# Gate and residual mixes as one pair of row halves in a slot of the gate and value ring

## The chip, the cores and the metric

The kernel runs on one core of one Trainium2 chip. The metric is the device time of one execution in microseconds (us), the median of several runs. Ratios are the mean time of one kernel's fast runs over that of the kernel before in the same rounds, so they are not quite the ratio of the medians quoted. Engines: PE (matmuls), DVE (vector), ACT (scalar and activations), POOL (general), SP (issues transfers).

## The reference, cut to what matters

An attention through 32 inducing points, then a gated feed-forward layer on 49,664 tokens of 128 channels (`mab(q, kv)` is a softmax attention of q over kv):

```
h   = mab(inducing, x)            # per batch of 4: 32 x 128
x   = mab(x, h)                   # weights rt (tokens x 32), times h
g   = x @ w_gate ; val = x @ w_val            # 128 -> 1536
ffn_out  = gelu(g) * val @ w_out              # 1536 -> 128
res_gate = sigmoid(x @ w_res)
out = x + res_gate * ffn_out
```

The kernel never forms x of the second attention for the big products: as x = rt @ h, it folds h into the weights (`hg`, `hv`, `hr`) and multiplies them by `rt`. Two small products per group remain, the *mixes*: `rt @ hr` for the gate (as a tanh) and `rt @ ha` for the residual.

## The kernel before

A group is 512 tokens. It has six gate and six value tiles of 128 x 1024, in a ring of three PSUM tiles of two banks each. The other two of the eight banks, the side banks, hold the output sums of even and odd groups, and, when free, the mixes and other small work.

```python
ps_gv = ...tile_pool(name="psgv", bufs=3, space=PSUM)       # the ring
ps_2 = [...tile_pool(name=f"ps{i}", bufs=1, space=PSUM) for i in range(2)]

def side_bank(group): return ps_2[group % 2].tile(...)
def misc_bank():      return side_bank(parity[0] + 1)
def wide_bank():      return ps_gv.tile([P, 2 * TOK], ...)

def gate_slot(gi, si):            # v: two 64-row matmuls, one per row half
    v = slot_mms(gi, si, hg_t)
    act.activation(ge[:, :n], v, AC.Gelu, ...)                # L331
def value_slot(gi, si):
    v = slot_mms(gi, si, hv_t)                                # L322
    ve.tensor_tensor(u[:, :n], ge_t.pop((gi, si)), v, AL.mult) # L338
# class Last, one per group
def mms(self, n): ...             # 8 of 48 output matmuls, L361
def mix(self, h):                 # L370, rows 0 to 63
    bank = side_bank(self.gi + 1)
    r = slice(0, 2 * M)
    for k in range(self.nk):
        pe.matmul(bank[:, k * P:(k + 1) * P], rt...[r, self.j0 + k, :], h[r, :], ...)
def gate(self):      ...tanh of mix(hr) into th               # L378
def residual(self):  ...copy of mix(ha) into at               # L384
def end(self):
    ve.scalar_tensor_tensor(th, th, 1.0, ffn, AL.add, AL.mult)  # L389
    po.tensor_tensor(at, at, th, AL.add); sy.dma_start(out..., at)
...
# f: the group's first window; one gate, one value and one window per step
for i in range(6):
    at(f + 2 + i, lambda lg=lg: lg.mms(8))
at(f + 5, lg.gate, START)
at(f + 6, lg.residual, START)
at(f + 7, lg.end, LATE)
```

A window is the place in the program's order behind each value, where other pieces of work are put. Gates run up to four ahead of values. In a window the pieces go in the order START, MIDDLE, END, LATE. In batches 0 to 2 the groups also carry work for the next batch: a burst of exponentials, then sums in the side banks (`accumulate`, L172), then a second burst. A quiet stretch is one without such work, above all in batch 3.

The softmax here doesn't subtract the row's maximum and nothing guards it: scores larger than these inputs give would overflow.

## Time and profile before

| | before |
|---|---|
| median of 3 runs | 857.97 us (857.3 to 858.31) |
| a quiet group, start to start of L389 | 7.76 us |
| DVE's own work in it (6 x 1.131 + 0.598) | 7.39 us |

Here are the busy times of one quiet group, from L389 to the next L389 (the columns are the length, then each engine's busy time and its number of instructions).

```profile
core 0: us, PE busy (x) PEld busy (x) DVE busy (x) ACT busy (x) POOL busy (x), PEclk, DMA share, GB/s
749.79:757.55 7.76, 7.52 (x83) 4.47 (x82) 7.56 (x9) 6.97 (x9) 1.27 (x1) 1.00 0.09 35
```

PE and DVE both look 97% busy. But the recorded time of an instruction reaches into the next one: DVE starts a product every 1.131 us although each lasts 1.21. Start to start is what counts here. The view of waits has PE's value and gate matmuls wait little for ACT:

```profile
PE gv L322 <- ACT ge L331: 11.7, 34, 1.1
```

### The profile page before, as it was taken

To read this page: it belongs to the slowest core of one execution; us is meant where nothing else is said; L and a number is where in the kernel's file an instruction comes from. 1 tells how busy PE (TensorE), PEld (TensorE's weight loads), DVE (VectorE), ACT (ScalarE), POOL (GpSimd) and SP (SyncE) were. 2 spreads that over 40 slices of the span, in tenths; PEclk is the share of its full clock that TensorE was granted. 3 is DMA by queue.
4 is the path that set the end of the run, shared out by engine and by line. 5 is a ranking of instruction groups with operands and counts; after the bars stand their busy time and mean duration, and the time that the engine had idled before them with its cause. 6 is when DMAs were issued, how large, how long until landed. Compare 5 with 4: busy or idle time off the path is not lost.

```text
span 855.8 us, 23356 instructions
## 1 busy us (share of the span) xinstructions
PE 795.1 (93%) x9602; PEld 479.1 (56%) x9602; DVE 796.7 (93%) x784; ACT 734.1 (86%) x861; POOL 356.9 (42%) x313
## 2 busy tenths in 40 slices
PE   5889999999899999999989999999989999999997
PEld 4545556555555555555555555555555555555554
DVE  8699999899999999899999999989999999999997
ACT  5599998888889989888989998988888999988994
POOL 2538885111468766112247867311245611111111
PEclk9599999999999999999999999999999999999999
DMA  8337874010447765101245876200135501010111
GB/s 308 110 85 157 207 176 121 27 38 27 84 96 165 182 172 127 40 26 38 51 88 106 221 163 161 74 31 27 38 64 100 116 26 39 38 39 27 38 38 41
DMA packets 123787, 79.42 MB, mean 93 GB/s; under 512 B 102016, under 2 KB 104736, under 8 KB 123680
## 3 DMA queue, kind: packets, MB, share of 16 engines
q1 hardware_dynamic: 121392, 75.50, 35.4%
q10 hardware_dynamic: 2288, 2.43, 1.0%
q8 instruction: 75, 1.23, 0.7%
q14 instruction: 32, 0.26, 0.1%
HBM read 27.87 MB, written 25.43 MB: 62 GB/s over the span
## 4 chain that ended last, share of the span: by engine, by line
PE 52%; DVE 25%; issue 11%; ACT 8%; DMA 1%; POOL 1%; DVEq 0%; ACTq 0%; POOLq 0%; SPq 0%
PE gv L322 26%; DVE u L338 19%; PE sb L361 19%; ACT ge L331 6%; PE sb L370 5%; DVE lo L123 2%; DVE th L389 1%; DVE z L275 1%; DVE hi L121 1%; PE sb L172 1%; ACT at L384 1%; ACT th L378 1%; DMA ge<-in_moe_w_out_dram 1%; PE sb L174 0%; POOL wO L450 0%
## 5 line engine op out<-in xcount | busy, mean ns | idle before, releaser
L338 DVE TENSOR_TENSOR u<-ge,gv 128x1024 bf16<-128x1024 f32 x584 | 691.1, 1213 | 41.8 <-PE gv L322 26.0
L331 ACT ACTIVATE ge<-gv 128x1024 f32<-128x1024 f32 x584 | 591.7, 1023 | 79.3 <-PE gv L322 67.0
L361 PE MATMUL sb<-wO,u 128*128 128x128 bf16 x4656 | 360.5, 220 | 0.1
L361 PEld LDWEIGHTS <-u 128*128 128x128 bf16 x4656 | 262.1, 98 | 121.4 <-issue 98.9
L392 POOL TENSOR_TENSOR at<-at,th 128x512 f32<-128x512 f32 (+1 forms) x100 | 123.8, 1238 | 407.6 <-ACT ge L331 369.4
L322 PE MATMUL gv<-rt,hv 64*128 64x512 f16 x1152 | 222.5, 378 | 25.6 <-ACT ge L331 9.7
L322 PE MATMUL gv<-rt,hg 64*128 64x512 f16 x1152 | 224.9, 385 | 11.7 <-DVE u L338 6.9
L322 PEld LDWEIGHTS <-hv 64*128 64x128 bf16 x1200 | 99.5, 94 | 103.0 <-issue 88.6
L322 PEld LDWEIGHTS <-hg 64*128 64x128 bf16 x1200 | 63.9, 93 | 76.6 <-issue 16.8
L289 POOL TENSOR_TENSOR a<-e,z 128x1024 f16<-128x1024 f32 (+2 forms) x50 | 91.2, 1832 | 20.8 <-ACT e2s L268 12.9
L370 PEld LDWEIGHTS <-rt 64*128 64x128 f16 x768 | 56.7, 93 | 37.9 <-issue 17.6
L123 POOL TENSOR_TENSOR lo<-xf,hi 128x1024 f16<-128x1024 f32 x36 | 76.8, 2134 | 0.3
L389 DVE SCALAR_TENSOR_TENSOR th<-th,sb 128x512 f32<-128x512 f32 (+1 forms) x100 | 66.4, 664 | 1.8 <-PE sb L361 1.8
L378 ACT ACTIVATE th<-sb 128x512 f32<-128x512 f32 (+1 forms) x100 | 57.9, 579 | 8.8 <-PE sb L370 8.6
L384 ACT ACTIVATE at<-sb 128x512 f32<-128x512 f32 (+1 forms) x100 | 58.0, 580 | 0.8 <-PE sb L370 0.8
L121 POOL CAST hi<-xf 128x1024 f16<-128x1024 f32 x36 | 37.3, 1037 | 22.6 <-DMA xf<-in_x_dram 19.1
L370 PE MATMUL sb<-ha,rt 64*128 64x128 f16 x384 | 36.5, 214 | 0.2
L370 PE MATMUL sb<-hr,rt 64*128 64x128 f16 x384 | 36.6, 215 | 0.0
L148 PEld LDWEIGHTS <-xt 128*128 128x128 f16 x768 | 23.8, 98 | 3.3 <-issue 2.3
L139 ACT ACTIVATE xt<-gv 128x1024 f16<-128x1024 f16 x12 | 12.3, 1024 | 13.4 <-PE gv L138 13.3
L138 PE MATMUL gv<-identF,hi 128*128 128x128 f16 x96 | 11.2, 288 | 9.0 <-DVE hi L121 8.9
L268 ACT ACTIVATE e<-gv 128x1024 f32<-128x1024 f32 (+2 forms) x13 | 11.9, 959 | 7.8 <-PE gv L148 7.8
(93 smaller groups left out, 259.0 us busy)
## 6 DMA issues: line engine op xcount, KB each, us to landing
out_dram<-at SPq DMA_DIRECT2D x96, 256.0 KB, 2.1
xf<-in_x_dram SPq DMA_DIRECT2D x42, 512.0 KB, 4.2
ge<-in_x_dram SPq DMA_DIRECT2D x6, 512.0 KB, 5.8
rt<-a SPq DMA_TRANSPOSE x49, 3.1
xt<-hi SPq DMA_TRANSPOSE x36, 3.3
ge<-in_moe_w_gate_dram ACTq DMA_DIRECT2D x1, 512.0 KB, 4.8
ge<-in_moe_w_val_dram ACTq DMA_DIRECT2D x1, 512.0 KB, 4.3
ge<-in_moe_w_out_dram ACTq DMA_DIRECT2D x1, 512.0 KB, 4.4
```

What stands on the lines that cost most here:

```text
L121: e_hi.tensor_copy(hi[:, :w, :], xf[:, :w, :])
L123: e_lo.tensor_tensor(lo[:, :w, :P], xf[:, :w, :], hi[:, :w, :], AL.subtract)
L289: po.tensor_tensor(a2[:, :n], ev[:, o:o + n, :].unsqueeze(2).to_broadcast([P, n, Q, M]), z[:, 1, o:o + n].unsqueeze(2).unsqueeze(3).to_bro ...
L322: pe.matmul(v[:, c * tw:(c + 1) * tw], weights[b][r, (c0 + c) * P:(c0 + c + 1) * P], rt[r, :], start=True, stop=True)
L331: act.activation(ge[:, :n], v, AC.Gelu, bias=0.0, scale=1.0)
L338: ve.tensor_tensor(u[:, :n], ge_t.pop((gi, si)), v, AL.mult)
L361: pe.matmul(self.ffn[:, k, :], u_t[self.gi, si][:, o:o + P], wO[:, fc, :], start=first, stop=not self.todo, skip_group_check=True)
L370: pe.matmul(bank[:, k * P:(k + 1) * P], rt_t[self.b, self.k][r, self.j0 + k, :], h[r, :], start=True, stop=True)
L378: act.activation(self.th[:, :self.tw], bank[:, :self.tw], AC.Tanh, bias=0.0, scale=0.5)
L384: act.activation(self.at[:, :self.tw], bank[:, :self.tw], AC.Copy, bias=0.0, scale=1.0)
L389: ve.scalar_tensor_tensor(self.th[:, :tw], self.th[:, :tw], 1.0, self.ffn.rearrange("p k c -> p (k c)")[:, :tw], AL.add, AL.mult)
L392: po.tensor_tensor(self.at[:, :tw], self.at[:, :tw], self.th[:, :tw], AL.add)
```

## The change

The intent is to take the two mixes out of PE's way, run them in both row halves at once, and read them while DVE is on the final product. The mixes get a tile of the ring of their own, one window earlier than the group's first output matmuls.

```diff
-        po.tensor_tensor(ha[M:2 * M, :], hf[M:2 * M, :], ha[M:2 * M, :], AL.subtract)
+        po.tensor_tensor(ha[3 * M:, :], hf[3 * M:, :], ha[3 * M:, :], AL.subtract)
...
-        def mix(self, h):
-            bank = side_bank(self.gi + 1)
-            ... (and gate(), residual(), each with its own mix)
+        def mix(self):
+            bank = wide_bank()
+            n = self.tw
             for k in range(self.nk):
+                for r, o, h in ((slice(0, 64), 0, hr_t), (slice(64, 128), TOK, ha_t)):
+                    pe.matmul(bank[:, o + k * P:o + (k + 1) * P],
+                              rt_t[self.b, self.k][r, self.j0 + k, :], h[self.b][r, :], ...)
+            act.activation(self.th[:, :n], bank[:, :n], AC.Tanh, bias=0.0, scale=0.5)
+            act.activation(self.at[:, :n], bank[:, TOK:TOK + n], AC.Copy, ...)
...
+        at(f + 1, lg.mix, END)
...
-            at(f + 5, lg.gate, START)
-            at(f + 6, lg.residual, START)
... (and the two like them for the short group at the end of a batch)
```

In the kernel after, the lines are L372 (mix), L376 (tanh), L378 (copy), L382 (final product) and L385 (POOL's sum).

More of the change, by code (lines that the diff above doesn't have):

```diff
@@ L364, in mms @@
                     del u_t[self.gi, si]
-        def mix(self, h):
-            bank = side_bank(self.gi + 1)
-            r = slice(0, 2 * M)
+        def mix(self):
+            bank = wide_bank()
+            n = self.tw
             for k in range(self.nk):
-                pe.matmul(bank[:, k * P:(k + 1) * P],
-                          rt_t[self.b, self.k][r, self.j0 + k, :],
-                          h[r, :], start=True, stop=True)
-            return bank
-        def gate(self):
-            bank = self.mix(hr_t[self.b])
+                for r, o, h in ((slice(0, 64), 0, hr_t), (slice(64, 128), TOK, ha_t)):
+                    pe.matmul(bank[:, o + k * P:o + (k + 1) * P],
+                              rt_t[self.b, self.k][r, self.j0 + k, :], h[self.b][r, :],
+                              start=True, stop=True)
             self.th = p_fin.tile([P, TOK], FP32, name="th", tag="th")
-            act.activation(self.th[:, :self.tw], bank[:, :self.tw], AC.Tanh,
-                           bias=0.0, scale=0.5)
-        def residual(self):
-            bank = self.mix(ha_t[self.b])
+            act.activation(self.th[:, :n], bank[:, :n], AC.Tanh, bias=0.0, scale=0.5)
             self.at = p_fin.tile([P, TOK], FP32, name="at", tag="at")
-            act.activation(self.at[:, :self.tw], bank[:, :self.tw], AC.Copy,
-                           bias=0.0, scale=1.0)
+            act.activation(self.at[:, :n], bank[:, TOK:TOK + n], AC.Copy, bias=0.0, scale=1.0)
         def end(self):
@@ L513 @@
                 at(f + 2 + i, lambda lg=lg: lg.mms(8))
-            at(f + 5, lg.gate, START)
-            at(f + 6, lg.residual, START)
             at(f + 7, lg.end, LATE)
         else:
-            at(f + 2, lg.gate, START)
             at(f + 3, lambda lg=lg: lg.mms(len(lg.todo)))
-            at(f + 3, lg.residual, START)
             at(f + 3, lg.end, LATE)
```

## The prediction

> **What bounds the kernel now.** I read the page first, for the busy shares, the waits of the costly groups and the chain that ended last.
>
> ```profile
> PE 795.1 (93%) x9602; PEld 479.1 (56%) x9602; DVE 796.7 (93%) x784; ACT 734.1 (86%) x861; POOL 356.9 (42%) x313
> ...
> PE 52%; DVE 25%; issue 11%; ACT 8%; DMA 1%; POOL 1%; DVEq 0%; ACTq 0%; POOLq 0%; SPq 0%
> ...
> L338 DVE TENSOR_TENSOR u<-ge,gv 128x1024 bf16<-128x1024 f32 x584 | 691.1, 1213 | 41.8 <-PE gv L322 26.0
> L331 ACT ACTIVATE ge<-gv 128x1024 f32<-128x1024 f32 x584 | 591.7, 1023 | 79.3 <-PE gv L322 67.0
> ```
>
> PE and DVE are both 93% busy, ACT 86%, and the chain goes back and forth between PE, DVE and ACT. No single engine is the bound; what binds is a loop through the three-slot ring of wide PSUM tiles. So I read the timeline of a quiet stretch (750 to 766 us), where the last batch has no other work beside the groups. The columns are start, time, engine, line and operation.
>
> ```profile
> 752.78 0.39 PE L322 MATMUL gv<-rt,hg 64*128 64x512 f16 x2
> ...
> 753.21 0.39 PE L322 MATMUL gv<-rt,hv 64*128 64x512 f16 x2
> ...
> 753.42 0.38 PE L370 MATMUL sb<-hr,rt 64*128 64x128 f16 x4
> 753.73 0.45 PEld L361 LDWEIGHTS <-u 128*128 128x128 bf16 x8
> 753.73 0.62 PE L361 MATMUL sb<-wO,u 128*128 128x128 bf16 x8
> 754.18 0.59 ACT L378 ACTIVATE th<-sb 128x512 f32<-128x512 f32 x1
> 754.28 0.10 PEld L322 LDWEIGHTS <-hg 64*128 64x128 bf16 x2
> 754.29 0.39 PE L322 MATMUL gv<-rt,hg 64*128 64x512 f16 x2
> ...
> 755.64 0.59 ACT L384 ACTIVATE at<-sb 128x512 f32<-128x512 f32 x1
> ...
> 756.12 2.12 ACT L331 ACTIVATE ge<-gv 128x1024 f32<-128x1024 f32 x2
> ...
> 756.41 1.22 DVE L338 TENSOR_TENSOR u<-ge,gv 128x1024 bf16<-128x1024 f32 x1 [0.18 <-PE gv L322]
> ...
> 757.55 0.68 DVE L389 SCALAR_TENSOR_TENSOR th<-th,sb 128x512 f32<-128x512 f32 x1
> ```
>
> The final product (L389) starts at 757.55 and again at 765.30: a group of 512 tokens takes 7.76 us. Read start to start, a product L338 costs DVE 1.131 us and L389 0.598, so DVE alone needs 6 x 1.131 + 0.598 = 7.39 us. The missing 0.37 is idle DVE before the last product of one group and the second of the next. Both follow the mixes: L370 stands in PE's order between a value pair and the output matmuls, 0.31 us each time, and the second mix also waits until ACT has read the first. The intent is to remove these two delays, and a gap-free DVE would give 7.39 us.
>
> **What the Trainium skill says.** "TensorE: Matmul & The Clock Gate", The mechanism: matmuls stay in strict order, and those of different row groups overlap. The trace agrees: two 64-row L322 matmuls together take 0.39 us, while the four L370 matmuls, all in rows 0 to 63, step by 0.078 us. "TensorEngine Tiling (Array Packing)", Key Properties: changing the tiling mode drains TensorE. The trace agrees: from value pair to mix 0.21 us, from value pair to L361 0.32. "Perfetto Trace Analysis", Identifying Performance Opportunities: the same bubble repeating can mean that there isn't enough PSUM for the next tile. Here the 0.18 us bubble repeats in each group, and what I expect after the change is a larger one of the same kind.
>
> **The change part by part.** Call a group's gate and value tiles G0..G5 and V0..V5, its eight output matmuls after each value M, and the new mix X. The gates run four ahead. The order of the built program is, from the fourth window on: G7 V3 M, G8 V4 M, G9 V5 M, then next group's G10 V0 M, G11 V1 M X, G12 V2 M, G13 V3.
>
> (1) Removed from PE: two mixes of 4 x 0.078 = 0.31 us and the waits on the side bank. Added: one X of eight matmuls in alternate row halves, and one more change of tiling mode is not needed (X is followed by a gate pair). If the halves overlap, X lasts 0.31 us, at the pace of single ones 0.62; I take 0.45. PE's work is then 6 x 1.09 (pair 0.22, pair 0.32, M 0.55) plus M-to-X within it, plus X: about 7.0 us. Alone that is no bound.
>
> (2) ACT does the same tanh and copy, 0.48 us from start to start each (at to ge at 755.64 and 756.12), but now one after the other. Its work, 6 x 0.921 + 0.96 = 6.5 us, is no bound either.
>
> (3) POOL and DVE do the same. The moved low part of the residual operand costs nothing.
>
> (4) The ring now carries 13 tiles in a group, not 12, with three buffers. Each tile waits for the one three earlier. Before, every gate waits for a value (freed by DVE) and every value for a gate (freed by ACT). After: X waits for V0, G12 for G11, V2 for V1, G13 for X, and **V3 waits for G12, whose gelu stands behind X's tanh and copy in ACT's queue**. I checked these waits in the built program's order: the gate behind X waits on ACT, the next value on DVE, the next gate and value on ACT.
>
> The path that returns to itself after one group, with its measured steps:
> - V3 to M to G8: 0.32 + 0.55 = 0.87 us (750.54, 750.86; 753.73, 754.29).
> - G8 to its gelu 0.43 to 0.48, gelu 1.025, release to V5 0.05: 1.51 to 1.56 (a gate at 755.69 freed a value at 757.20; another 751.65 and 753.21). I take 1.53.
> - V5 to M to G10: 0.87. G10, gelu, V1: 1.53.
> - V1 to M to X: 0.87.
> - X to tanh: seven to eight matmuls at 0.04 to 0.078, plus 0.21 for the last and 0.04: 0.5 to 0.8, I take 0.6. Tanh and copy 0.96. Gelu of G12 1.03, release to V3 0.05. Sum 2.64.
>
> Total 3 x 0.87 + 2 x 1.53 + 2.64 = **8.31 us**, against 7.76 now: +0.55 in a quiet group. DVE is not in this path; its 7.39 us would leave it 11% idle. The mix no longer delays PE, but makes a full turn of a ring of three, with 0.96 us of ACT work in it and a gelu behind it.
>
> The sum over the run, with group times from the starts of L389:
> - Batch 0, 56 to 143 us, 11 groups of 7.95 on average (waits for other work are in them already): about +0.4 each, +4.
> - Batches 1 and 2, 11 groups each of 7.82: +0.5, +11.
> - Batch 3, 22 groups of 7.81: +0.5 or a little more, +12.
> - The three stretches with accumulation (154 to 223 us and its repeats), 24 groups of 8.6: the accumulation is 0.69 us of PE between V3 and M (172.88 to 173.57), so in the new path too, but not in every group. New time about 9.0: +0.4, +10.
> - About 12 groups around the bursts of exponentials, which DVE and ACT work bounds: +0.3, +4.
> - Start and tail: 0.
>
> Together +41: 858 + 41 = **899 us**.
>
> **The rivals.** (a) The intent works: no mix between value and output matmuls, DVE without gaps. The gain would be 0.37 x 94 groups = 34 us, to about 824. For it: both engines' idle time before L338 stems from the mixes, and X starts while DVE has 0.60 us of L389 to do. Against: L389 covers 0.60 us, but tanh, copy and the gelu behind them take 2 us, and V3's matmuls can't start before; from V0's product (start 0, freed 1.26) X, tanh, copy, gelu, V3 and DVE's 0.49 us wait come to 4.4 us, where DVE would be there at 3.99. (b) X's weight loads do not overlap, and PE becomes the bound: 7.2 us at most by the count in (1), under the ring's path; it adds 0.15 at X, +14 us, to about 913. (c) The buffers of the residual: X takes one a whole group earlier, and ACT's copy then waits for the store of two groups before. The store lands 4.1 us after L389 in quiet stretches, where the new order leaves 8.6; but in batch 0, between 72 and 135 us, it lands 7.5 to 13.0 us after, as POOL is behind with conversions. Slower groups let POOL catch up; up to +8 us, not in my sum. (d) The shorter PE work and lost waits offset the new ones: about 858. That needs X's way through ACT to be 0.5 us shorter, and I find no step that could be.
>
> **Range and chances.** X to tanh leaves 0.2 us either way per group, some 15 us in all; how much of the loss the busy stretches hide, 10 us; rival (c) adds on one side only. Range 876 to 924. Faster 0.06: only if the order of waits that I read is wrong. Same 0.11. Slower 0.83.
>
> **What would show it.** In the quiet stretch of the new profile: L389 starts 8.2 to 8.5 us apart (right), 7.4 (intent), 7.7 (offset). In the waits, PE gv L322 behind ACT ge grows from 11.7 us to some 80 or more, most of it at the value pair that comes second after X, and DVE u L338 behind PE gv from 26.0 to 70 or more. DVE's share falls to about 89%. The new mix's eight matmuls last 0.3 us if the halves overlap, 0.6 if not. Waits of at behind a DMA around 70 to 135 us would show (c). I am wrong if DVE runs on without a gap past L389 and V2, or if PE waits there on DVE and not on ACT.

## The result, and the profile after

The changed kernel took **914.51 us** (909.68 to 916.05, 4 runs) against 858.14 us (4 runs) before: ratio 1.0646, 95% interval 1.0604 to 1.0688. It is 6.5% slower.

The page of the kernel after, in the lines that answer to those of before:

```profile
PE 799.9 (87%) x9602; PEld 455.5 (50%) x9602; DVE 805.9 (88%) x784; ACT 740.0 (81%) x861; POOL 357.9 (39%) x313
...
DVE 43%; PE 22%; ACT 18%; issue 8%; DMA 4%; POOL 3%; DVEq 0%; ACTq 0%; SPq 0%; POOLq 0%
...
L338 DVE TENSOR_TENSOR u<-ge,gv 128x1024 bf16<-128x1024 f32 x584 | 695.8, 1215 | 90.8 <-PE gv L322 75.9
...
L322 PE MATMUL gv<-rt,hv 64*128 64x512 f16 x1152 | 226.6, 384 | 77.9 <-ACT ge L331 38.9
```

All engines are busy for a smaller share; DVE's idle time ahead of the products grew from 41.8 to 90.8 us. The chain now names DVE first. I took this for a tie, as DVE runs right behind PE and a walk back can go through DVE's products or through PE and ACT; nothing tests that, and I went by the timeline. One quiet group, 801.97 to 810.73 us:

```profile
801.97 0.62 PE L361 MATMUL sb<-wO,u 128*128 128x128 bf16 x8
...
802.53 0.23 PE L372 MATMUL gv<-hr,rt 64*128 64x128 f16 x1
802.53 0.23 PE L372 MATMUL gv<-ha,rt 64*128 64x128 f16 x1
...
803.02 0.60 ACT L376 ACTIVATE th<-gv 128x512 f32<-128x512 f32 x1 [0.34 <-PE gv L372]
...
803.52 0.59 ACT L378 ACTIVATE at<-gv 128x512 f32<-128x512 f32 x1
...
804.00 1.95 ACT L331 ACTIVATE ge<-gv 128x1024 f32<-128x1024 f32 x2
...
805.08 0.39 PE L322 MATMUL gv<-rt,hv 64*128 64x512 f16 x2 [0.39 <-ACT ge L331]
...
805.58 5.99 DVE L338 TENSOR_TENSOR u<-ge,gv 128x1024 bf16<-128x1024 f32 x5 [0.44 <-PE gv L322]
...
805.96 0.39 PE L322 MATMUL gv<-rt,hg 64*128 64x512 f16 x2
...
807.46 0.39 PE L322 MATMUL gv<-rt,hv 64*128 64x512 f16 x2
...
809.85 0.39 PE L322 MATMUL gv<-rt,hv 64*128 64x512 f16 x2
```

This is the predicted loop, step by step. Mix X at 802.53, tanh 803.02, copy 803.52, gelu of the gate behind X 804.00 (its end frees a buffer at 805.03), value V3 at 805.08. From there G8 at 805.96, V5 at 807.46 when G8's gelu ends, and V1 of the next group at 809.85 when the gelu of the second gate after that ends; the next X stands at 810.73. A group takes **8.20 us** instead of 7.76, 0.44 more. DVE stands still for 0.44 us before V3's product, behind PE, which waited for ACT. (That the two figures are equal is chance: against DVE's own 7.39 us the group now loses 0.81, before it lost 0.37.) The same group by busy time:

```profile
core 0: us, PE busy (x) PEld busy (x) DVE busy (x) ACT busy (x) POOL busy (x), PEclk, DMA share, GB/s
803.28:811.48 8.20, 7.48 (x80) 4.07 (x80) 7.70 (x8) 7.01 (x9) 1.27 (x1) 1.00 0.08 32
```

No engine has more to do than before, within 0.14 us; the group became longer by waiting alone.

Where the 58.5 us between the two profiled runs (spans 855.8 and 914.3) arose, by the starts of the final products:

| stretch | before | after | more |
|---|---|---|---|
| start to first final product | 56.1 | 60.2 | 4.1 |
| batch 0, 11 groups | 87.4 | 96.1 | 8.7 |
| batches 1 and 2, 12 groups each | 94.1, 94.1 | 104.5, 101.0 | 17.3 |
| batch 3, 24 groups | 186.3 | 198.7 | 12.4 |
| accumulation, 3 times 8 groups | 68.7 each | 73.3, 73.4, 73.3 | 13.9 |
| bursts of exponentials, ends of batches, tail | | | 2.1 |

The first row looks like scatter of the start (55.2 to 60.2 in the runs, most of whose kernels are alike up to there). The second and third hold something besides the loop: in batch 0 one group took 10.97 us, and at the start of batch 1 one took 12.30 us.

```profile
275.08 0.60 ACT L378 ACTIVATE at<-gv 128x512 f32<-128x512 f32 x1 [2.50 <-DMA out_dram<-at]
...
275.73 0.39 PE L322 MATMUL gv<-rt,hg 64*128 64x512 f16 x2 [2.63 <-ACT at L378]
```

ACT's copy waits until the store of two groups before has left its buffer `at`, and PE waits behind ACT. That is the prediction's rival (c), at another place than it named: the last group of a batch is one block long and takes 3.1 us, so "two groups before" is close.

### The profile page after: what moved, and what is told of

Its sections match the earlier page's. It is cut to its first block, busy times and chain, and to the rows that moved or that the text cites. A ratio compares the mean times of both kernels' runs of the same rounds, so it can differ in the third digit from the quotient of the medians.

```text
span 914.3 us, 23267 instructions
## 1 busy us (share of the span) xinstructions
PE 799.9 (87%) x9602; PEld 455.5 (50%) x9602; DVE 805.9 (88%) x784; ACT 740.0 (81%) x861; POOL 357.9 (39%) x313
## 4 chain that ended last, share of the span: by engine, by line
DVE 43%; PE 22%; ACT 18%; issue 8%; DMA 4%; POOL 3%; DVEq 0%; ACTq 0%; SPq 0%; POOLq 0%
DVE u L338 39%; ACT ge L331 12%; PE gv L322 11%; PE sb L361 7%; ACT at L378 4%; DMA xf<-in_x_dram 2%; DMA out_dram<-at 2%; DVE th L382 1%; DVE lo L123 1%; POOL lo L123 1%; POOL a L289 1%; DVE hi L121 1%; POOL at L385 1%; PE gv L372 1%; DVE z L275 1%
## 5 line engine op out<-in xcount | busy, mean ns | idle before, releaser
L338 DVE TENSOR_TENSOR u<-ge,gv 128x1024 bf16<-128x1024 f32 x584 | 695.8, 1215 | 90.8 <-PE gv L322 75.9
L331 ACT ACTIVATE ge<-gv 128x1024 f32<-128x1024 f32 x584 | 584.5, 1026 | 98.4 <-PE gv L322 86.3
L361 PEld LDWEIGHTS <-u 128*128 128x128 bf16 x4656 | 265.0, 98 | 147.4 <-issue 144.1
L385 POOL TENSOR_TENSOR at<-at,th 128x512 f32<-128x512 f32 (+1 forms) x100 | 123.7, 1238 | 461.4 <-ACT at L378 318.3
L322 PE MATMUL gv<-rt,hv 64*128 64x512 f16 x1152 | 226.6, 384 | 77.9 <-ACT ge L331 38.9
L376 ACT ACTIVATE th<-gv 128x512 f32<-128x512 f32 (+1 forms) x100 | 58.4, 584 | 39.3 <-PE gv L372 38.3
L382 DVE SCALAR_TENSOR_TENSOR th<-th,sb 128x512 f32<-128x512 f32 (+1 forms) x100 | 66.3, 664 | 0.0
L378 ACT ACTIVATE at<-gv 128x512 f32<-128x512 f32 (+1 forms) x100 | 58.0, 580 | 5.4 <-DMA out_dram<-at 5.4
L372 PE MATMUL gv<-hr,rt 64*128 64x128 f16 x384 | 38.0, 220 | 2.2 <-DVE u L338 2.2
L372 PE MATMUL gv<-ha,rt 64*128 64x128 f16 x384 | 38.1, 220 | 0.0
L372 PEld LDWEIGHTS <-rt 64*128 64x128 f16 x768 | 22.2, 95 | 12.3 <-issue 2.4
L139 ACT ACTIVATE xt<-gv 128x1024 f16<-128x1024 f16 x12 | 12.3, 1023 | 14.6 <-PE gv L138 14.4
```

The costliest lines, as they stand in the source:

```text
L322: pe.matmul(v[:, c * tw:(c + 1) * tw], weights[b][r, (c0 + c) * P:(c0 + c + 1) * P], rt[r, :], start=True, stop=True)
L331: act.activation(ge[:, :n], v, AC.Gelu, bias=0.0, scale=1.0)
L361: pe.matmul(self.ffn[:, k, :], u_t[self.gi, si][:, o:o + P], wO[:, fc, :], start=first, stop=not self.todo, skip_group_check=True)
L372: pe.matmul(bank[:, o + k * P:o + (k + 1) * P], rt_t[self.b, self.k][r, self.j0 + k, :], h[self.b][r, :], start=True, stop=True)
L376: act.activation(self.th[:, :n], bank[:, :n], AC.Tanh, bias=0.0, scale=0.5)
L378: act.activation(self.at[:, :n], bank[:, TOK:TOK + n], AC.Copy, bias=0.0, scale=1.0)
```

## The experiments

**Theory:** the loop V3, M, G8, gelu, V5, M, G10, gelu, V1, M, X, tanh, copy, gelu, V3 sets the pace. **Rivals:** PE's work or its order alone; the placement beside L389; the residual's buffers; the thirteenth turn of the ring whatever ACT does. Eleven kernels ran, the first four in one job, the next four in a second and the last three in a third. Each job measured the kernel before again (857.98, 858.47 and 859.38 us).

| run | median us | ratio to before | quiet group us |
|---|---|---|---|
| changed kernel | 914.51 | 1.0646 | 8.20 |
| e1_short_copy | 877.7 | 1.0228 | 7.80 |
| e2_mix_first | 890.42 | 1.0377 | 7.84 |
| e3_at3 | 905.17 | 1.0543 | 8.20 |
| e4_before_early | 880.91 | 1.0255 | 7.63 |
| e5_rows0 | 930.01 | 1.0830 | 8.41 |
| e6_short_both | 865.35 | 1.0077 | 7.67 |
| e7_first_at3 | 882.15 | 1.0269 | 7.84 |
| e8_before_split | 857.16 | 0.9983 | 7.60 |
| e9_gate_early_th3 | 852.48 | 0.9922 | 7.58 |
| e10_gate_early_later | 851.5 | 0.9913 | 7.58 |
| e11_up6 | 911.78 | 1.0608 | 8.20 |

All are correct except e1 and e6. Their outputs are wrong, which doesn't matter for the times.

**e1_short_copy: take ACT time out of the loop.**

```diff
-            act.activation(self.at[:, :n], bank[:, TOK:TOK + n], AC.Copy, ...)
+            act.activation(self.at[:, :32], bank[:, TOK:TOK + 32], AC.Copy, ...)
-            po.tensor_tensor(self.at[:, :tw], self.at[:, :tw], self.th[:, :tw], AL.add)
+            po.tensor_tensor(self.at[:, :tw], self.th[:, :tw], self.th[:, :tw], AL.add)
```

> Changed kernel with the copy of the residual cut from 512 to 32 columns (result wrong on purpose; POOL adds th to th). Theory (the loop V3, M, G8, gelu, V5, M, G10, gelu, V1, M, X, tanh, copy, gelu, V3 sets the pace, 8.20 us in the quiet stretch): the copy's 0.48 us falls to about 0.08, so a quiet group takes about 7.80 us and the run about 914 - 0.40 x 80 = 882 us. Rival (PE's order and its work set the pace): no change of over 5 us.

877.7 us, the quiet group 7.80: the 0.40 us taken from the copy came off the group whole (8.20 to 7.80). PE's work is unchanged, so PE's work is not the bound; ACT's copy lies on the loop.

**e2_mix_first: shorten another step of the loop.**

```diff
-        at(f + 1, lg.mix, END)
+        at(f + 1, lg.mix, START)
```

> Changed kernel with the mix tile ahead of the window's output matmuls (START instead of END), so that X follows V1 by 0.22 us rather than 0.87, or as soon as V0's product frees its buffer (about 0.36 us earlier than now). Theory: the loop shortens by that, a quiet group takes about 7.84 us instead of 8.20 and the run about 886 us. Rival (the placement under L389 is what matters and an earlier X waits more on DVE): same or slower, 910 to 930.

890.42 us, the quiet group 7.84, as expected to the hundredth. In its timeline the mix comes ahead of the output matmuls, and the rest follows:

```profile
790.48 0.21 PE L372 MATMUL gv<-hr,rt 64*128 64x128 f16 x1
...
790.82 0.62 PE L361 MATMUL sb<-wO,u 128*128 128x128 bf16 x8
790.98 0.60 ACT L376 ACTIVATE th<-gv 128x512 f32<-128x512 f32 x1
```

So the place beside L389 was not the best one even for this form.

**e3_at3 and its control e11_up6: the residual's buffers.** There was no room for a third `at` without taking a buffer from `u`; e11 takes that one alone.

```diff
-    p_u = ...tile_pool(name="up", bufs=7)
+    p_u = ...tile_pool(name="up", bufs=6)
-            self.at = p_fin.tile([P, TOK], FP32, name="at", tag="at")
+            self.at = p_fin.tile([P, TOK], FP32, name="at", tag="at", bufs=3)   # e3 only
```

> Changed kernel with three buffers of the residual tile at, not two (one buffer fewer of u, which has seven and holds three or four). Theory: ACT's wait for the store (5.4 us in the profile) and PE's stall behind it at the start of a batch (2.6 us) go away; quiet groups stay at 8.20; the run is 5 to 10 us shorter, about 907. Rival (batch 0 and the batch starts are slow because of the ring alone): no change, 914.

> Control for the run with three residual buffers: changed kernel with six buffers of u and all else unchanged. Theory (u never holds more than four): no change, 914 as the changed kernel. Rival (u's buffers mattered): not 914.

e3 took 905.17 us, and in its trace ACT's copy never waits for a store; quiet groups stayed at 8.20, and the first groups of the batches took 8.42 each, where the changed kernel had 12.30 and 9.0. The control took 911.78 us (ratio 1.0608, the changed kernel 1.0646). By the ratios, the third buffer is worth 0.65% of 858, 5.6 us, against the control, and 8.8 us against the changed kernel; the intervals of e3 (1.0526 to 1.0561) and of the control (1.0582 to 1.0635) do not meet. This is a cause of its own beside the loop. It is in different stretches, which e7 checks.

**e7_first_at3: both mendings together.** The edit is that of e2 with that of e3.

> Changed kernel with both mendings that worked: mix tile ahead of the output matmuls, and three residual buffers. Theory: the two gains (24 us and 9 us) lie in different stretches and add: about 881 us, still slower than before, as ACT's tanh and copy are still on the loop (7.84 us). Rival (they overlap): 888.

882.15 us, ratio 1.0269: 32 us under the changed kernel, and 24 + 9 had been expected. The two add, and the form is still 2.7% slower than before. Its quiet group, 7.84, is only 0.08 us over the 7.76 of the kernel before, so the quiet loop is the smaller part of what is left. Of the 26.6 us between the two profiled spans, by the starts of the final products, 7.0 lie in the ends of the batches, 6.4 in batch 0, 6.3 in the accumulation stretches and 7.6 in the other groups of batches 1 to 3. In batch 0 one group took 12.59 us: with `at` free, tanh there waits 2.6 us for POOL's sum to release one of the two `th`.

**e5_rows0: undo the row halves, keep the slot.**

```diff
-                for r, o, h in ((slice(0, 64), 0, hr_t), (slice(64, 128), TOK, ha_t)):
+                for r, o, h in ((slice(0, 64), 0, hr_t), (slice(0, 64), TOK, ha_t)):
```

(The low part of `ha` goes back to rows 32 to 63.)

> Changed kernel with both mixes in rows 0 to 63 again (row halves undone, ring slot kept). Theory: the eight matmuls of X then step by 0.078 us and not in pairs by 0.057, so tanh starts about 0.3 us later after X, and X stands on the loop: a quiet group takes 8.5 us instead of 8.20, the run about 938. Rival (PE's work is not on the loop): 914.

930.01 us, the quiet group 8.41. Tanh starts 0.72 us after X, not 0.50, and the group is longer by that 0.21, not by the 0.3 that I had expected (a single mix matmul steps by 0.057 us, not 0.078). Within this slot the row halves are thus a gain of some 16 us; the loss comes from the slot in the ring, with tanh and copy on its way. No run puts the paired mixes into the side banks.

**e6_short_both: the turn of the ring with next to no ACT time.** Tanh and copy are both cut to 32 columns, and the final product reads a constant in place of tanh.

```diff
-            act.activation(self.th[:, :n], bank[:, :n], AC.Tanh, ...)
+            act.activation(self.th[:, :32], bank[:, :32], AC.Tanh, ...)
```

> Changed kernel with both the tanh and the copy cut to 32 columns (result wrong on purpose; the final product reads a constant in place of tanh). Theory: what hurts is ACT's 0.97 us on the loop, not the thirteenth turn of the ring by itself: the loop falls to about 7.4 us, level with DVE's own 7.39, so a quiet group takes 7.4 to 7.5 us and the run about 850, under the kernel before. Rival (a thirteenth tile in a ring of three costs by itself): over 7.7 us, 870 or more.

865.35 us, the quiet group 7.67, where I expected 7.4 to 7.5 and 850. Here the theory fell short. The timeline shows what stands under the first loop:

```profile
782.66 0.23 PE L372 MATMUL gv<-hr,rt 64*128 64x128 f16 x1
...
783.47 0.68 DVE L382 SCALAR_TENSOR_TENSOR th<-ident,sb 128x512 f32<-128x512 f32 x1
...
783.60 0.39 PE L322 MATMUL gv<-rt,hv 64*128 64x512 f16 x2
```

With thirteen tiles in a ring of three, the value V2 waits for the buffer of V1, the value just ahead of it, and that comes free only when DVE has read it (the product starts at 782.33, ends at 783.55, V2 starts at 783.60). From V1's matmuls at 781.80 to V2's is 1.80 us. From V2 on, PE and ACT need two windows for gate, gelu, value, output matmuls: 0.87 + 1.51 = 2.38 us, twice, and another 1.10 to the next V1 at 789.47: 7.67. So with almost no ACT work on the turn the group still takes 0.28 us over DVE's 7.39. This second loop is read from one trace; no run isolates it. But 7.67 is also 0.09 under the 7.76 of the kernel before: in quiet groups the turn by itself costs no more than the old mixes did, and ACT's tanh and copy on it make up the loss against that kernel. What e6 loses to it lies in batch 0 (7.2 us) and batch 1 (3.6 us): there ACT waited 8.1 us for the store in three groups, two of batch 0 and the first of batch 1, which took 9.9 to 13.7 us.

**e4_before_early: the kernel before, its mixes in earlier windows.** If the side-bank mixes hurt by where they stand, they can be moved without the ring.

```diff
-            at(f + 5, lg.gate, START)
-            at(f + 6, lg.residual, START)
+            at(f + 3, lg.gate, START)
+            at(f + 4, lg.residual, START)
```

> Kernel before with its two mixes three and two windows earlier (gate at f+3, residual at f+4), still in the side banks and rows 0 to 63. Theory for the kernel before: its two mixes lay on the path V1, DVE, L389, V2, G8, gelu, V5, mix, M, G10, V0, mix, M, G11, V1; between V3 and G8 PE waits for DVE anyway (0.2 us), so there they cost little: a quiet group takes 7.45 to 7.6 us instead of 7.76, the run about 838. Rival (a mix costs PE its 0.31 us wherever it stands): 7.76, 858.

880.91 us: a miss. Quiet groups did shrink, to 7.63. But each accumulation stretch grew from 68.7 to between 76.2 and 77.3 us. In it, PE's accumulation waits for ACT's tanh:

```profile
PE sb L172 <- ACT th L378: 4.0, 4, 1.2
```

By the code, `misc_bank` is the very side bank that the mix of the same group uses, and both now want it in the fourth window. Its late place had kept the mix out of the accumulation's way.

**e8_before_split: late in the groups with other work in the side banks, f+3 and f+5 in the rest.**

> Kernel before with the mixes at f+3 and f+5 in groups without accumulation or other work in the side banks, and where they were in the others. Theory: the kernel with both mixes early lost 8 us in each accumulation stretch, as the mix and the accumulation took turns in one side bank, and gained 0.13 us in each quiet group; with the second mix one window later its wait for tanh (0.2 us) goes too: quiet group 7.4 to 7.5 us, run 838 to 848, faster than the kernel before. Rival (the side bank is not why the accumulation stretches were slow): they stay 8 us longer than before.

857.16 us, ratio 0.9983 (0.9959 to 1.0006): the same as before. The accumulation stretches are back at 68.4 us, so the early place in these groups was the cause of e4's loss. That it acts through the shared bank is read from the code and from the 4.0 us of waits above, about half of the 8.6 lost in that stretch. But the quiet group takes 7.60, not 7.4 to 7.5, and in batch 0 one group took 12.3 us, as tanh waited 2.8 us for POOL to release `th`.

**e9_gate_early_th3 and e10_gate_early_later: one mix early, one late.** The gate mix goes to f+3 in groups without other work in the side banks, the residual mix stays at f+6. e9 has a third buffer of `th` (and one fewer of `u`); e10 leaves the buffers, and batch 0, as before.

```diff
+            g = gi % gpb
+            busy = gi < gpb or gi < (B - 1) * gpb and (13 <= g <= 20 or g == 23)   # e10
-            at(f + 5, lg.gate, START)
+            at(f + (5 if busy else 3), lg.gate, START)
```

> Kernel before with the gate mix at f+3 (where it was in groups with other work in the side banks) and the residual mix left at f+6, three buffers of th, one fewer of u. Theory: in a ring of three, a gate, its gelu and the value that takes its buffer make every second window a loop of 2.38 us; a mix in every second window of one phase adds its 0.21 us to that loop (both mixes at f+3 and f+5: 7.60 us a group), while with one mix in each phase each loop has only one, 6 x 1.19 + 0.21 = 7.35 us, under DVE's 7.39: quiet group 7.40 to 7.45 us, batch 0 no longer held up by th, run 840 to 846. Rival (the mix's cost does not depend on the phase): 7.60, 855 to 858.

> The same with the buffers as before and batch 0 left as before. Theory: quiet groups of batches 1 to 3 take 7.40 to 7.45 us, batch 0 as before; run 843 to 849. Rival: 7.60, 855 to 858.

852.48 and 851.5 us, ratios 0.9922 and 0.9913 (e10: 0.9894 to 0.9931). These are the best kernels, by 0.9%, which is under the 2% that counts as faster. Both miss the 840 to 849 that I had expected. The quiet group takes 7.58, not 7.40: the idea that only the phase of the windows counts does not hold. Tanh and copy, 0.48 us each, still come ahead of a gelu in ACT's queue, which may be why; what bounds 7.58 was not taken apart further. Nor did e9's third `th` free batch 0: there ACT's copy stood 2.6 us behind a store that held `at`, and one group took 14.2 us.

## Why the prediction was right

The direction, the mechanism and the range (876 to 924) held; the time, 914.5, was in the upper part, 15 us over the 899 predicted.

- **What binds**, a loop through the ring and no single engine: shown for the new kernel, where e1 and e2 moved the time by shortening steps of the loop while PE's, DVE's and ACT's other work stayed. For the kernel before it stays a reading. Earlier mixes (7.63, 7.60, 7.58) took 0.13 to 0.18 us off the 0.37 that the prediction puts down to them, no more. That idle time, too, stands a little elsewhere than it says: before the first and the second product of a group (762.77 and 764.17, 0.10 and 0.27 late), not before the last.
- **The new loop**, with V3 waiting for a gelu that stands behind tanh and copy: right, step by step in the timeline. Predicted 8.31, measured 8.20. The term that was too large is X to tanh, 0.6 predicted and 0.50 measured. I had read the pace of a mix matmul as 0.31 / 4 = 0.078 us, but that 0.31 also holds the switch from half to full rows: in the trace before, the four start 0.055 us apart (761.18 to 761.35). The eight started within 0.18 us, in pairs 0.055 to 0.067 apart.
- **Cost of X on PE**: I took 0.45 us; it is 0.23 (802.53 to 802.76), as the halves overlap: the two of a pair start 0.004 us apart.
- **The sum over the run**, where the mis-sized terms are: batch 3 +12 predicted, +12.4 measured. This match is in part luck: 24 times the measured 0.44 is 10.6, and most of the other 1.8 come from groups that I had not priced, below. Batch 0 +4 against +8.7, batches 1 and 2 +11 against +17.3, the accumulation +10 against +13.9; the bursts +4 against 2.1 with the ends of batches and the tail; the start 0 against +4.1. I had given batch 0 less than a quiet group's loss, on the ground that its waits were for other work. In truth the three groups after each burst in which, by the code, the gates' lead grows by one lose more than a quiet one (8.34 became 9.0 to 9.1), and rival (c) came on top. Why an accumulation group lost 0.58 us was not taken apart.
- **Rival (c)**, the residual's buffers: set at up to 8 us and left out of the sum; e3 shows 5.6 to 8.8. I expected it in batch 0, where POOL lags; the trace has 1.9 us of ACT's wait there and 3.5 at the starts of batches.
- **Rival (a)**, the intent: a quiet group never came to 7.39. e6 shows that in this form it did not, even with nearly all of ACT's tanh and copy taken away: 7.67.
- **Rival (b)**, PE as the bound: out, by e1 and by X's 0.23 us. **Rival (d)**, an offset: out.
- **What would show it**: L389 (now L382) 8.20 apart, at the edge of 8.2 to 8.5; DVE 88%, said 89; DVE behind PE 75.9 us, said 70 or more. PE gv behind ACT ge did not reach 80: it is 39.9 us, with another 15.8 behind the copy:

```profile
PE gv L322 <- ACT ge L331: 39.9, 93, 0.7
...
PE gv L322 <- ACT at L378: 15.8, 28, 2.6
```

PE's idle time in this view is cut by matmuls whose modelled ends reach into the wait, so the sum of waits understates a delay that the starts show in full: V3 at 805.08 stands 0.78 us behind its gate, where two pairs without a wait are 0.22 apart, but is listed with 0.39.

## What to carry to other kernels

When work is moved into a shared ring, write down for each tile which earlier tile's buffer it takes and who frees that, and follow the loop once round: an added tile shifts who waits for whom, and whatever the freeing engine has queued in between lies on the loop. Judge by start to start in a quiet stretch, not by busy shares; here nobody had more to do and the time still rose by 6.5%. And a piece of work that looks misplaced may be there because its bank is free only then.

## What the Trainium skill lacked or had wrong

- "Perfetto Trace Analysis", Identifying Performance Opportunities, has repeating bubbles as a sign of too little PSUM. It lacks that the order of the tiles decides which engine frees a buffer, as each tile takes that of the tile one ring's length ahead: in a ring of three, gates and values in turn let values wait for ACT and gates for DVE; one tile more made a value wait for the value just ahead (at V2 in e6, a group of 7.67 us against DVE's 7.39) and another for a gelu behind tanh and copy (8.20).
- "TensorEngine Tiling (Array Packing)", Key Properties, says that a change of tiling mode drains TensorE, but gives no size: from a half-row pair to full-row matmuls the step was 0.32 us, to a half-row matmul 0.21 to 0.22, so about 0.10 us for a change (an estimate from these steps).
